# One small load moved to another queue, and the last projection partly issued earlier, in a decode-attention kernel limited by its loads

## The chip, the cores and the metric

The kernel runs on one core of a Trainium2 chip. The metric is device time of one execution in microseconds (us). A profiled execution also has a *span*, from the core's first to its last instruction; here the time is 1.8 to 1.9 us longer than the span throughout. In the record a run is *fast* or *slow*: slow when it is over 1.5% above the fastest of the same kernel. Engines: PE (TensorE), DVE (VectorE), ACT (ScalarE), POOL (GpSimd) and SP (SyncE, which here issues DMA transfers and computes nothing). PEld is PE's weight load, SPq and ACTq are the DMA issuing of SP and ACT.

## The reference

Eight tokens pass through two branches that a gate mixes. Branch A is attention with one query per token over the last 1,024 entries of a cache; branch B is a small MLP.

```python
q = (x @ wq) -> [8 tokens, 16 heads, 256]
k, v = last 1024 of the caches [8, 8 kv heads, 4096, 256], each for 2 query heads
o = softmax(q k^T / 16) v              # per token and head
a = o.reshape(8, 16 * 256) @ wo        # [4096, 448]
b = gelu(layernorm(x) @ w1 + b1) @ w2 + b2
g = sigmoid((x * gate_w).sum(-1))
out = g * a + (1 - g) * b              # [8, 448] bf16
```

All is bf16. Keys and values are 67 MB of the 77.7 MB that have to be read, so this is a kernel that reads memory.

## The kernel before

All large loads are issued by SyncE, in one order, into a ring of nine slots of 2 MB. `pump()` issues loads as long as slots are free; `done()` frees one. A unit `u` is four kv heads of one token; there are 16 units. For each, PE transposes the keys, computes scores, DVE and ACT do the softmax, PE multiplies by the values. At the start and the end the program says:

```python
x_sb = consts.tile([NB, D], BF16)
nc.sync.dma_start(x_sb[:], xf)         # 7 KB, first on SyncE
pump()                                 # nine slots; keys of unit 0 come first, in two halves
...
nc.scalar.dma_start(gw_b[:], ...)      # small constants on ScalarE
...
bring(u); values(u - 1)                # u = 15, the last unit
A_ps = ps_misc.tile([P, DQ], F32, ...); nc.vector.memset(A_ps[:], 0.0)
finish(u - 1)                          # head outputs 0-7 of token 7 complete
values(u); finish(u)                   # head outputs 8-15 of token 7
# "spread": 16 small matmuls bring all head outputs into the layout of wo's rows
for i in range(HPQ):
    for m in range(HPQ):
        nc.tensor.matmul(pp[32 * i : 32 * i + 32, m], lhsT=ident[:, m::HPQ], rhs=oTv[:, i], ...)
nc.vector.tensor_copy(oP[:], ...)
for q in range(NHQ):                   # projection with wo, 4 x 32 matmuls
    ...
nc.vector.scalar_tensor_tensor(res[:], in0=A_ps[:], ...)   # gate and mix
for i, (src, cols) in enumerate(quads(res)):               # four stores of 1.8 KB
    eng = nc.sync if i % 2 == 0 else nc.scalar
    eng.dma_start(out_f[:, cols], src)
```

wo's last quarter is loaded in three pieces, so that only the last 8 of 128 projection matmuls need the last bytes. The four stores alternate between SyncE and ScalarE, so SyncE's last two transfers are stores.

## Time and profile before

| | before |
|---|---|
| time, median of 3 (range) | 197.02 us (196.73 to 197.06) |
| span of the profiled run | 195.0 us |
| busy: PE, DVE, ACT | 76%, 58%, 43% |
| read by the large loads | 77.67 MB |
| share of DMA in the chain of waits | 96% |

From the page of the kernel before: granted PE clock (tenths), busy tenths of the 16 DMA engines, and what they moved, in 40 slices of 4.9 us.

```profile
...
PEclk9997566999999999999999999999999999999655
DMA  4999999999999999999999999999999999999940
GB/s 165 426 425 408 444 421 427 408 424 424 430 424 430 420 430 427 427 427 424 425 424 430 427 427 417 425 424 424 417 424 430 427 430 420 427 424 407 413 151 3
...
```

Read from left to right: after the first slice the DMA engines are full at about 425 GB/s up to the third last slice. In the second last the share drops to 4 tenths, and the last slice is empty. From the same page, the chain of work that ended last, by engine and by line:

```profile
...
DMA 96%; SPq 1%; issue 0%; PE 0%; DVE 0%
DMA slot<-in_A_k_cache_dram 58%; DMA slot<-in_A_v_cache_dram 20%; DMA slot<-in_A_wo_dram 10%; DMA slot<-in_A_wq_dram 7%; SPq L107 1%; SPq L123 1%; PE A_ps L562 0%; SPq L172 0%; DVE res L569 0%
...
```

From the last instruction backwards, each step is a landing of a large load that waited for the one before it. PE, DVE and ACT hardly occur in it.

The start in the timeline (start us, duration us, engine, line, operation, count):

```profile
...
0.73 0.58 ACTq L177 DMA_DIRECT2D gw_b<-in_gate_w_dram  x1
...
0.73 0.38 SPq L172 DMA_DIRECT2D x_sb<-in_A_x_dram  x1
...
1.17 1.27 SPq L107 DMA_DIRECT2D slot<-in_A_k_cache_dram  x2
...
```

x goes out first on SyncE, and the first key load 0.44 us later. The end in the timeline of the same run:

```profile
...
187.00 3.05 PE L562 MATMUL A_ps<-slot,oP 128*8 128x112 bf16 x120 [0.55 <-DVE oP L555]
190.27 0.36 PE L562 MATMUL A_ps<-slot,oP 128*8 128x112 bf16 x8 [0.22 <-DMA slot<-in_A_wo_dram]
...
190.68 0.33 DVE L569 SCALAR_TENSOR_TENSOR res<-A_ps,gg_s,mixb 128x112 bf16<-128x112 f32 x1 [3.73 <-PE A_ps L562]
191.04 1.05 SPq L579 DMA_DIRECT2D out_dram<-res  x2
191.04 0.67 ACTq L579 DMA_DIRECT2D out_dram<-res  x2
```

In the square brackets stands the idle time of the engine before the group, and what ended it. PE does 120 of the projection's matmuls, waits 0.22 us for the last bytes of wo, does the last 8; then DVE mixes, and SyncE and ScalarE store.

### The profile page before, as it was taken

The page shows a single profiled execution, that of the slowest core. Times are in us where ns is not written, and L with a number is a line of the kernel's source. Part 1 is how long each engine was busy: PE and PEld are TensorE (multiplying, and loading weights), DVE is VectorE, ACT ScalarE, POOL GpSimd, SP SyncE. Part 2 cuts the span into 40 slices and gives each one's busy share as a digit, 9 for nine tenths or more (in the row PEclk, how much of TensorE's full clock was granted, in tenths as well). Part 3 has the DMA queues.
Part 4 walks back from the last instruction along what each step waited for, and adds up shares of the span by engine and source line. Part 5 has one row for each costly group of instructions (what it writes and reads, how often), then busy time and mean ns, then how long its engine had stood idle before and what let it go on. Part 6 is the DMA issues. An engine that isn't in the chain of part 4 may idle for free.

```text
span 195.0 us, 5167 instructions
## 1 busy us (share of the span) xinstructions
PE 148.3 (76%) x2318; PEld 110.5 (57%) x2318; DVE 112.6 (58%) x258; ACT 82.9 (43%) x101; POOL 0.9 (0%) x7
## 2 busy tenths in 40 slices
PE   1399967887778787878767878778787878994780
PEld 0399927755565656564636464647373737553570
DVE  7531342867575757575738484847575757777210
ACT  2362003636373727272708181818282828562000
POOL 1000000000000000000000000000000000000000
PEclk9997566999999999999999999999999999999655
DMA  4999999999999999999999999999999999999940
GB/s 165 426 425 408 444 421 427 408 424 424 430 424 430 420 430 427 427 427 424 425 424 430 427 427 417 425 424 424 417 424 430 427 430 420 427 424 407 413 151 3
DMA packets 6744, 78.02 MB, mean 400 GB/s; under 512 B 945, under 2 KB 1346, under 8 KB 1986
## 3 DMA queue, kind: packets, MB, share of 16 engines
q1 hardware_dynamic: 6528, 77.67, 94.7%
q8 instruction: 18, 0.29, 0.6%
q10 hardware_dynamic: 194, 0.02, 0.1%
q14 instruction: 4, 0.03, 0.0%
HBM read 77.68 MB, written 0.01 MB: 398 GB/s over the span
## 4 chain that ended last, share of the span: by engine, by line
DMA 96%; SPq 1%; issue 0%; PE 0%; DVE 0%
DMA slot<-in_A_k_cache_dram 58%; DMA slot<-in_A_v_cache_dram 20%; DMA slot<-in_A_wo_dram 10%; DMA slot<-in_A_wq_dram 7%; SPq L107 1%; SPq L123 1%; PE A_ps L562 0%; SPq L172 0%; DVE res L569 0%
## 5 line engine op out<-in xcount | busy, mean ns | idle before, releaser
L325 ACT COPY kt<-ktp 128x1024 bf16<-128x1024 bf16 x64 | 63.2, 1017 | 82.1 <-PE ktp L322 82.1
L322 PE MATMUL ktp<-ident,slot 128*128 128x128 bf16 x1024 | 71.2, 226 | 21.6 <-ACT kt L325 10.9
L322 PEld LDWEIGHTS <-slot 128*128 128x128 bf16 x1024 | 64.8, 103 | 28.4 <-issue 15.6
L327 DVE COPY kt<-ktp 128x1024 bf16<-128x1024 bf16 x64 | 41.3, 685 | 16.0 <-PE ktp L322 16.0
L360 PE MATMUL S_ps<-kt,qw 128*8 128x512 bf16 x256 | 32.4, 627 | 0.3 <-DVE qw L351 0.3
L372 DVE TENSOR_REDUCE nmx<-S_ps 128x1 f32<-128x1024 f32 x16 | 19.6, 1225 | 22.4 <-PE S_ps L360 22.4
L388 DVE STREAM_TRANSPOSE EB<-E 128x1024 bf16<-128x1024 bf16 x16 | 19.9, 1245 | 6.3 <-ACT E L380 6.1
L420 PE MATMUL PO<-slot,ET 128*8 128x256 bf16 x512 | 17.6, 282 | 6.1 <-DVE ET L401 6.1
L380 ACT ACTIVATE E<-S_ps,nmx 128x1024 bf16<-128x1024 f32 x16 | 17.9, 1120 | 2.4 <-DVE nmx L373 2.4
L420 PEld LDWEIGHTS <-ET 128*8 128x8 bf16 x512 | 11.4, 88 | 10.3 <-DVE ET L401 8.4
L360 PEld LDWEIGHTS <-qw 128*8 128x8 bf16 x256 | 7.3, 95 | 12.0 <-issue 10.4
L401 DVE CAST ET<-sm 128x256 bf16<-128x256 f32 x16 | 6.7, 417 | 0.5 <-PE sm L399 0.5
L396 PE MATMUL sm<-EB,perm 128*128 128x256 bf16 x16 | 4.4, 273 | 1.6 <-DVE EB L388 1.6
L399 PE MATMUL sm<-selr,ones_f 128*128 128x8 f32 x32 | 5.3, 237 | 0.0
L440 DVE CAST oT<-sm 128x16 bf16<-128x16 f32 x16 | 3.5, 221 | 2.8 <-PE sm L437 2.8
L399 PEld LDWEIGHTS sm<-selr,ones_f 128*128 128x128 f32 x32 | 4.8, 188 | 0.1
L562 PE MATMUL A_ps<-slot,oP 128*8 128x112 bf16 x128 | 3.4, 295 | 0.8 <-DVE oP L555 0.5
L339 PE MATMUL qt<-xT,slot 128*128 128x8 bf16 x128 | 3.6, 168 | 0.4 <-DVE z L470 0.4
L339 PEld LDWEIGHTS <-slot 128*128 128x128 bf16 x128 | 3.6, 104 | 0.4 <-issue 0.3
L562 PEld LDWEIGHTS <-oP 128*8 128x8 bf16 x128 | 2.9, 121 | 1.2 <-DVE oP L555 0.7
L470 DVE TENSOR_TENSOR z<-hT,b_sb 128x112 f32<-128x112 f32 x1 | 0.3, 275 | 5.5 <-PE hT L460 5.5
L380 ACT ACTIVATION_READ_ACCUMULATOR E<-S_ps,nmx 128x1 f32 x16 | 3.2, 202 | 0.0
(122 smaller groups left out, 71.9 us busy)
## 6 DMA issues: line engine op xcount, KB each, us to landing
slot<-in_A_v_cache_dram SPq DMA_DIRECT2D x16, 2048.0 KB, 38.9
slot<-in_A_k_cache_dram SPq DMA_DIRECT2D x15, 2048.0 KB, 39.4
slot<-in_A_wo_dram SPq DMA_DIRECT2D x3, 896.0 KB, 32.0
slot<-in_A_k_cache_dram SPq DMA_DIRECT2D x2, 1024.0 KB, 7.1
slot<-in_A_wq_dram SPq DMA_DIRECT2D x1, 2048.0 KB
slot<-in_B_w_dram SPq DMA_DIRECT2D x1, 1568.0 KB
slot<-in_B_w_dram SPq DMA_DIRECT2D x1, 1344.0 KB, 9.8
slot<-in_A_wq_dram SPq DMA_DIRECT2D x1, 1024.0 KB
```

The costliest lines, as they stand in the source:

```text
L322: nc.tensor.transpose(ktp[:, c, :], kn[:, o : o + P], ident[:])
L325: nc.scalar.copy(dst, ktp[:])
L327: nc.vector.tensor_copy(dst, ktp[:])
L339: nc.tensor.matmul(qt[:, k, :], lhsT=w[:, o + c : o + c + P], rhs=xT[:, r + half, :], start=(r == 0 and k == 0), stop=(r == NR), skip_grou ...
L360: nc.tensor.matmul(S_ps[32 * a : 32 * a + RQ, hf * CH * SK : (hf + 1) * CH * SK], lhsT=qw[:, j, b, half, a, :], rhs=KT[hf][:, j, :, a::QUA ...
L372: nc.vector.reduce_max(nmx[:], S_ps[:], axis=AXIS.X, negate=True)
L380: nc.scalar.activation(E[:], S_ps[:], ACT.Exp, bias=nmx[:], scale=1.0, accum_out=rowsum[:])
L388: nc.vector.transpose(EB[:].rearrange("p c r -> p (c r)"), E[:])
L399: nc.tensor.matmul(sm[:, NCK, :], lhsT=ones_f[:], rhs=selr[:], start=True, stop=True)
L401: nc.vector.tensor_copy(ET[:], sm[:, 0:NCK, :])
L420: nc.tensor.matmul(PO[32 * t : 32 * t + RQ, :], lhsT=ET[:, c, 0:RQ], rhs=vn[:, c * Dh : (c + 1) * Dh], start=(c < QUAD), stop=(c >= NCK - ...
L562: nc.tensor.matmul(dst, lhsT=oP[:, j, q, :], rhs=w[:, o + cols.start : o + cols.stop], start=(q == 0 and j == 0), stop=(q == NHQ - 1 and j ...
```

## The change

Its intent: start the stream of loads earlier by taking x out of its queue, and take two waits of PE off the end by spreading and projecting the finished heads early.

```diff
     x_sb = consts.tile([NB, D], BF16)
-    nc.sync.dma_start(x_sb[:], xf)
     pump()
+    nc.scalar.dma_start(x_sb[:], xf)
...
     finish(u - 1)
-    values(u)
-    finish(u)
-    pp = ps_sm.tile(...)          # spread of all heads, one cast
...
+    def spread_rows(q0, q1): ...  # the same for a range of heads, pp from the ps_kt pool
+    def project(q): ...           # a quarter of the projection, as before
+
+    HALF = NHQ // 2
+    spread_rows(0, HALF)          # heads 0-7, complete by now
+    values(u)
+    finish(u)
+    project(0)
+    spread_rows(HALF, NHQ)
+    for q in range(1, NHQ):
+        project(q)
```

More of the change, by code (lines that the diff above doesn't have):

```diff
@@ L539, with spread_rows, project @@
     finish(u - 1)
-    values(u)
-    finish(u)
-    pp = ps_sm.tile([P, HPQ, NJ, NHQ, NB], F32, tag="sm", name="pp")
+    oP = consts.tile([P, NJ8, NHQ, NB], BF16)
     oTv = oT[:].rearrange("p (q i) j b -> p i j q b", i=HPQ)
-    for i in range(HPQ):
-        for m in range(HPQ):
-            nc.tensor.matmul(
-                pp[32 * i : 32 * i + 32, m],
-                lhsT=ident[:, m::HPQ],
-                rhs=oTv[:, i],
-                start=True,
-                stop=True,
-            )
-    oP = consts.tile([P, NJ8, NHQ, NB], BF16)
-    nc.vector.tensor_copy(oP[:], pp[:].rearrange("p m j q b -> p (m j) q b"))
-    for q in range(NHQ):
+    def spread_rows(q0, q1):
+        pp = ps_kt.tile([P, HPQ, NJ, q1 - q0, NB], F32, tag="ktp", name="pp")
+        for i in range(HPQ):
+            for m in range(HPQ):
+                nc.tensor.matmul(
+                    pp[32 * i : 32 * i + 32, m],
+                    lhsT=ident[:, m::HPQ],
+                    rhs=oTv[:, i, :, q0:q1, :],
+                    start=True,
+                    stop=True,
+                )
+        nc.vector.tensor_copy(
+            oP[:, :, q0:q1, :], pp[:].rearrange("p m j q b -> p (m j) q b")
+        )
+    def project(q):
         w = slot("wo", q - q % 2)
```

## The prediction

> **What bounds the kernel now.** The stream of big loads. The chain of waits is 96% DMA: keys 58%, values 20%, wo 10%, wq 7%. The queue table has 77.67 MB on the SyncE queue, 94.7% of sixteen engines' span; the page's slices show 9 tenths of DMA nearly throughout, near 425 GB/s[...]. PE is busy 76%, DVE 58%, ACT 43%; in the waits view PE waits 9.8 us for keys in 14 pieces, so it catches up with the loads again and again.
>
> So only three things can shorten the time: when the stream starts, how dense it is, and what follows its last byte.
>
> **Start.** In the timeline SyncE issues x at 0.73 us (0.38 us), and the first key half only at 1.17 us. The windows view shows no large traffic until 2.5 us. The change takes x out of this queue: the first key issue should move to 0.73 us, and the whole stream with it, by 0.44 us. x goes out at 0.73 us on ScalarE instead and should land at 2.0 to 2.8 us (PE first needs it at 2.38 us today). A few tenths of delay in the norm and the first transposes (9.0 us) are absorbed.
>
> **Tail.** Today the last wo bytes land at 190.23 us. PE ends the first 120 projection matmuls at 190.05 us, waits 0.22 us for DMA, then does the last 8 (0.36 us), then comes res (0.33 us), the output, and the end at 195.0. So PE has 0.2 us of slack: nearly critical, not quite. The change adds 16 small matmuls (16 took 0.45 us) and one cast (at most 0.42 us). It buys away two waits of PE after the last value product: 0.32 us for oT and 0.55 us for oP are covered by project(0) and project(1) (about 0.8 us each). Against that come a wait of some 0.3 us for oT ahead of the early spread, and its matmuls. Net I estimate PE 0.2 to 0.4 us earlier. The instruction order has only a quarter of the projection ahead of the second spread, after the last value product. PE's chain begins with the landing of the 15th key block (waited for at 160.78 us), so it moves with the stream. The end stays with DMA: the tail part is worth nothing, at most 0.1 us in runs in which PE happens to be last.
>
> **Sum.** 197.02 - 0.44 - (0 to 0.1) = 196.5 us, eight in ten between 196.1 and 196.95. Faster by over 2%: 0.01; within 2%: 0.98; slower: 0.01.
>
> **What would show it.** Right: first key issue near 0.73 us, big traffic from near 2.1 us; last wo landing near 189.8 us; PE's wait for wo before the last 8 matmuls above 0.3 us; landing to end unchanged (4.8 us). Wrong on the start: the stream begins earlier but the last landing does not. Wrong on the tail: PE has no wait for wo at the end.
>
> **What would make it wrong.** The granted clock falls to 0.5 at about 181 us; if it falls earlier, PE becomes last and eats the gain. The end is also uneven: the DMA share falls from 0.94 at 182 to 186 us to 0.12 at 189 to 190 us, so a few engines finish last, and anything that delays one of them by some tenths counts as much as the change. Runs of the same kernel differ by 0.3 us.

## The result, and the profile after

| | before | after |
|---|---|---|
| time, median of 6 (range) | 196.85 us (196.59 to 197.06) | 195.52 us (195.46 to 195.63) |
| span of the profiled run | 195.0 us | 193.7 us |

The ratio of the fast runs is 0.9933 (95% interval 0.992 to 0.9946). Here and below a ratio is the mean time of one kernel's fast runs over the mean of the other's in the same rounds, so it is not quite the ratio of the medians quoted. The gain is 1.33 us; I had predicted 0.44 to 0.54 us, and the time lies below my range. It is a small gain, but with six runs on either side and no overlap it is not noise.

From the page of the changed kernel, the clock and DMA lines and the chain that ended last:

```profile
...
PEclk9998559999999999999999999999999999999555
DMA  5999999999999999999999999999999999999950
...
DMA 82%; PE 9%; ACT 3%; DVE 2%; issue 1%; SPq 1%; ACTq 0%
...
```

DMA still fills the middle; in the third last slice the clock is 5 instead of 6 tenths. The chain is 82% DMA instead of 96%: from 160.7 us on, the landing of the 15th key block, it runs through PE, ACT and DVE, so in this run PE's work, not the last load, ended last, if only just: `res` starts 0.45 us after the last landing of wo, as before. That was one of the risks that I had named; the second trace below does not show it.

The start of the changed kernel in the timeline:

```profile
...
0.73 0.60 ACTq L173 DMA_DIRECT2D x_sb<-in_A_x_dram  x1
...
0.73 1.28 SPq L107 DMA_DIRECT2D slot<-in_A_k_cache_dram  x2
...
```

As predicted, the first key load is issued 0.44 us earlier. Two lines of the windows view show the traffic of it, first of the kernel before, then of the changed one (stretch and its length, busy time of PE, PEld, DVE, ACT and POOL with counts, clock, DMA share, GB/s):

```profile
...
2.00:3.00 1.00, 0.39 (x5) 0.31 (x5) 0.88 (x7) 0.98 (x1) 0.00 (x0) 1.00 0.63 132
3.00:6.00 3.00, 0.13 (x2) 0.04 (x1) 2.31 (x13) 0.67 (x3) 0.00 (x0) 1.00 0.95 373
...
```

```profile
...
2.00:3.00 1.00, 0.40 (x5) 0.32 (x5) 0.88 (x7) 0.60 (x1) 0.00 (x0) 1.00 0.92 229
3.00:6.00 3.00, 0.13 (x2) 0.04 (x1) 2.31 (x13) 1.05 (x3) 0.00 (x0) 1.00 0.98 402
...
```

Summed from the trace's packets, the changed kernel's loads are 0.19 MB ahead at 6 us, which at 425 GB/s is 0.45 us; from 9 us on and until 184 us the lead is 0.25 to 0.31 us (0.10 to 0.13 MB). The end of the changed kernel in the timeline:

```profile
...
187.97 2.46 PE L563 MATMUL A_ps<-slot,oP 128*8 128x112 bf16 x96
...
190.48 0.33 DVE L580 SCALAR_TENSOR_TENSOR res<-A_ps,gg_s,mixb 128x112 bf16<-128x112 f32 x1 [1.92 <-PE A_ps L563]
190.84 0.71 SPq L590 DMA_DIRECT2D out_dram<-res  x2
190.84 0.65 ACTq L590 DMA_DIRECT2D out_dram<-res  x2
```

DVE starts to mix at 190.48 instead of 190.68 us: 0.20 us of the 1.27 us by which the spans differ. The remaining 1.07 us come after it, in a part that the change does not touch. SyncE now issues its two stores in 0.71 us instead of 1.05 us. And they land sooner. In the waits view of SyncE, its wait for the stores at the program's end (us in total, times, longest), before and after:

```profile
...
SPq L605 <- DMA out_dram<-res: 1.8, 2, 1.2
...
```

```profile
...
SPq L616 <- DMA out_dram<-res: 1.1, 2, 0.9
...
```

Times of the two ends, from the trace's records (us from the span's start):

```
                                        before    after
last wo landing                         190.23   190.03
first SyncE store issued                191.04   190.84
idle between the two SyncE stores         0.43     0.04
second SyncE store issued               191.78   191.25
last packet of it, and last but one     193.06, 192.62    192.14, 192.11
8 KB instruction fetch (one packet)     192.76-193.07     192.61-193.12
last store landed                       193.92   192.64
end of the span                         194.95   193.68
```

So there are two new facts. In the kernel before, SyncE pauses 0.43 us between two stores, though `res`, from which it stores, was ready at 191.01 us and the first store had been issued from it at 191.04. And one of that store's eight data packets starts at 193.06 us, 0.44 us after the last of the seven others; a fetch of 8,192 bytes of instructions, on some DMA engine, ends at 193.07 us.

### The profile page after: what moved, and what is told of

It is laid out like the page before. It is cut to its first block, busy times and chain, and to the rows that moved or that the text cites. A ratio compares the mean times of both kernels' runs of the same rounds, so it can differ in the third digit from the quotient of the medians.

```text
span 193.7 us, 5200 instructions
## 1 busy us (share of the span) xinstructions
PE 148.1 (76%) x2334; PEld 110.3 (57%) x2334; DVE 112.9 (58%) x259; ACT 82.7 (43%) x101; POOL 0.8 (0%) x7
## 4 chain that ended last, share of the span: by engine, by line
DMA 82%; PE 9%; ACT 3%; DVE 2%; issue 1%; SPq 1%; ACTq 0%
DMA slot<-in_A_k_cache_dram 77%; DMA slot<-in_B_w_dram 5%; ACT kt L325 2%; PE S_ps L360 2%; PE ktp L322 2%; PE PO L420 2%; PE A_ps L563 2%; ACT E L380 1%; PE sm L437 1%; SPq L107 1%; DVE EB L388 1%; DVE nmx L372 1%; PE sm L399 0%; PE sm L396 0%; PE pp L547 0%
## 5 line engine op out<-in xcount | busy, mean ns | idle before, releaser
L322 PE MATMUL ktp<-ident,slot 128*128 128x128 bf16 x1024 | 70.2, 224 | 22.1 <-ACT kt L325 11.4
L322 PEld LDWEIGHTS <-slot 128*128 128x128 bf16 x1024 | 63.7, 102 | 29.0 <-issue 15.7
L420 PE MATMUL PO<-slot,ET 128*8 128x256 bf16 x512 | 18.5, 290 | 6.4 <-DVE ET L401 6.4
L420 PEld LDWEIGHTS <-ET 128*8 128x8 bf16 x512 | 12.2, 90 | 10.5 <-DVE ET L401 8.7
L339 PEld LDWEIGHTS <-slot 128*128 128x128 bf16 x128 | 3.6, 104 | 0.4 <-issue 0.3
L403 DVE RECIPROCAL rb<-sm 128x8 f32<-128x8 f32 x16 | 3.2, 199 | 0.0
```

The lines of the kernel that those rows point to most:

```text
L322: nc.tensor.transpose(ktp[:, c, :], kn[:, o : o + P], ident[:])
L339: nc.tensor.matmul(qt[:, k, :], lhsT=w[:, o + c : o + c + P], rhs=xT[:, r + half, :], start=(r == 0 and k == 0), stop=(r == NR), skip_grou ...
L420: nc.tensor.matmul(PO[32 * t : 32 * t + RQ, :], lhsT=ET[:, c, 0:RQ], rhs=vn[:, c * Dh : (c + 1) * Dh], start=(c < QUAD), stop=(c >= NCK - ...
```

## The experiments

The theories at the outset: **S**, the gain comes from x leaving the SyncE queue, by way of the stores at the end; **E**, it comes from the new order of the projection, which changes when the end falls. My prediction's own terms (0.44 us for the start, nothing for the projection) are tested by the same runs. All kernels gave correct results.

### 1 to 4: each part alone, and both kernels again

The head part alone (`e1_head_only`):

```diff
-    nc.sync.dma_start(x_sb[:], xf)
     pump()
+    nc.scalar.dma_start(x_sb[:], xf)
```

> Only the first part of the change: keys issued first, x on the ScalarE queue; the end of the kernel as before. Theory S (x leaving the SyncE queue frees the output stores at the end: in the profile before, the second SyncE store was issued 0.43 us after the first had finished issuing and its last packet landed at 193.92 us, 0.86 us after the others; in the profile after, neither happened): about 195.7 us, and a span of about 193.9. Theory E (the stores' delay comes from how the end of the kernel falls, so from the projection part): about 196.6 us, a fall of 0.3 us at most, the head start of the stream, with the late store still there.

The tail part alone (`e2_tail_only`) is the changed kernel with this undone.

> Only the second part: early spread and projection of the first quarter between the value product and the second spread; x on SyncE ahead of the keys as before. Theory S: about 196.7 us, the late second store still there. Theory E: about 195.7 us, no late store. My prediction had this part at 0 to 0.1 us.

Both kernels unchanged, for a second trace:

> The kernel before, unchanged, for a second trace. If the late second SyncE store (0.43 us gap between the two SyncE store issues, last packet 0.86 us after the others) belongs to the kernel and is not chance, it is here again and the span is about 195.0 us; if it is chance, the span may be 194.0.

> The changed kernel, unchanged, for a second trace. If the early end of the stores belongs to the kernel, the four stores are issued within 0.75 us and the end comes 2.9 us after the first is issued, again; span about 193.7 us. Open too: whether PE again has no wait for wo at the end (granted clock down to 0.5 from about 178 us).

| run | time, median (range) | ratio to before (95%) | gap between SyncE's stores | first store to last landing |
|---|---|---|---|---|
| head part alone | 195.50 (195.43 to 195.85) | 0.9935 (0.992 to 0.995) | 0.04 us | 1.81 us |
| tail part alone | 196.70 (196.61 to 196.87) | 0.9994 (0.9977 to 1.0011) | 0.46 us | 2.63 us |
| before, again | 197.07 (one run) | | 0.46 us | 2.72 us |
| after, again | 195.90 (one run) | | 0.04 us | 1.81 us |

(In the first profiled runs: before 0.43 and 2.88 us, after 0.04 and 1.81 us. The record calls the state of the two single runs unknown; their traces, not their times, are used below.) The stores in the timeline of the two halves, first the head part alone, then the tail part alone:

```profile
...
190.89 0.70 SPq L579 DMA_DIRECT2D out_dram<-res  x2
```

```profile
...
191.25 1.08 SPq L590 DMA_DIRECT2D out_dram<-res  x2
```

The gain is in the head part alone, as far as can be measured; none is measurable in the tail part. E has fallen. The slow end is not chance: of these six traces it is in all three with x on SyncE, and in none without.

### 5 to 7: is it the transfer of x, or the place of the store in SyncE's program?

Taking x off SyncE does two things: it removes a transfer from a queue, and it makes SyncE's instruction stream shorter by one (89 records of SyncE in the trace after, 90 before). Counted from 0 in the built program, SyncE's second store is number 80 in the kernel before, and number 79 with x on ScalarE. Theory **P**: the number counts, because something at a fixed place in SyncE's instruction stream, between 79 and 80, holds it up (this place is called the boundary below). Theory **Q**: the transfer counts. A drain on SyncE (an instruction with no DMA, placed after the first nine slots of loads) separates the two.

```diff
     nc.scalar.dma_start(x_sb[:], xf)
+    nc.sync.drain(fusable=False)       # e5_head_drain1: one; e6_head_drain2: two
```

> The head part alone (195.5 us) plus one drain on SyncE after its first nine slots of loads: one instruction more in SyncE's program, no DMA[...]. SyncE's second store is then again its instruction number 80, as in the kernel before (79 with the head part alone). Theory P (what counts is the place of the last store in SyncE's instruction stream): the gap of 0.4 us between the two SyncE stores is back, and a late last packet, about 196.5 us. Theory Q (what counts is the x transfer itself on the SyncE queue[...]): no gap, 195.5 us.

> The same with two drains. Theory P in the form of a boundary in the instruction stream just ahead of number 80: the boundary now falls ahead of the first store, where SyncE waits over 10 us for the result anyway, so the gap is hidden and the time is back at about 195.5 us. If instead every further instruction costs, about 196.5 us or more. Theory Q: 195.5 us.

```diff
     nc.sync.dma_start(x_sb[:], xf)     # the kernel before
     pump()
+    nc.sync.drain(fusable=False)       # e7_before_drain1
```

> The kernel before, x on SyncE first, plus one drain on SyncE: nothing but one instruction added. Theory P with the boundary: the stores come without the gap and the kernel is faster by about 1 us, 195.8 us; what is left against the head part alone (195.5 us) is the worth of the earlier start of the stream, 0.25 to 0.44 us. Theory Q: no change, 196.8 us, or slower.

| run | number of 2nd store | time, median (range) | ratio to before (95%) | gap | 8 KB fetch | first store to last landing |
|---|---|---|---|---|---|---|
| head, one drain | 80 | 196.78 (196.48 to 196.88) | 1.0003 (0.9986 to 1.002) | 0.44 | 192.43-192.76 | 2.59 us |
| head, two drains | 81 | 196.00 (195.66 to 196.13) | 0.9959 (0.9944 to 0.9974) | 0.06 | 183.93-184.26 | 1.81 us |
| before, one drain | 81 | 195.91 (195.87 to 196.04) | 0.9958 (0.9943 to 0.9973) | 0.06 | 184.30-184.63 | 1.81 us |

The stores in the timeline of the three runs, in this order:

```profile
...
190.99 1.12 SPq L580 DMA_DIRECT2D out_dram<-res  x2
```

```profile
...
191.53 0.71 SPq L581 DMA_DIRECT2D out_dram<-res  x2
```

```profile
...
191.30 0.67 SPq L580 DMA_DIRECT2D out_dram<-res  x2
```

P holds and Q has fallen. One idle instruction more undoes the gain; two bring most of it back; and the kernel before becomes 0.9 us faster by an instruction that does nothing. The fetch marks the same place. Counted in each trace's own records of SyncE (which leave out branches), it begins 1.06 to 1.41 us after the end of the 79th record (the first store in the kernel before), whatever that record is, and 3.6 to 3.8 us after it in the two runs with number 81, in which the stream of loads is still running. With the second store at 79 the boundary comes after the stores, where SyncE waits for their landing anyway (in the changed kernel the fetch begins at 192.61 us, the last store lands at 192.64). At 80 it comes between the two stores: there SyncE pauses (0.43 us in the kernel before), and the fetch itself, from 192.76 to 193.07 us there, falls among the packets of the second store, from 192.56 to 193.08. At 81 the boundary lies ahead of the first store, where SyncE has to wait for the result anyway (11.2 and 10.7 us in its waits view); the fetch is then seen at about 184 us.

In all four traces with number 80 (before twice, tail alone, head with one drain) the last packet of the second store starts when the fetch ends, to 0.01 us: 193.06 and 193.07, 193.42 and 193.42, 193.15 and 193.16, 192.76 and 192.76. In the others the store's packets have gone before the fetch begins, or (number 81) the fetch ended some 8 us ahead of them. So the cost has at least two parts: SyncE's pause of 0.43 to 0.46 us, and the meeting with the fetch that comes with the pause (the last packet starts 0.12 to 0.44 us after the last of the others, at most 0.03 us without it). A third part has no explanation here: the landing is seen 0.69 to 0.83 us after the end of the last packet, against 0.48 to 0.56 us in the other traces. Together, from first store to last landing, 2.59 to 2.88 us against 1.79 to 1.83 us in the nine other traces of normal speed, 0.9 us in the mean.

I had expected 195.5 us for two drains, and got 196.0. In both runs with number 81 the fetch now lies inside the stream of loads, and wo landed late, at 190.71 and 190.57 us. That the fetch delayed the stream is a possible reason; no run tests it.

### 8, 9, 11, 12: what is the earlier start worth by itself?

A partner with the late start but the good end: x first on SyncE, and the first keys as one load, so that the second store is number 79 (`e8_x_first_k0_one`).

```diff
-    add_kv("k", A_k_cache, 0, parts=2)
+    add_kv("k", A_k_cache, 0)
```

> x first on SyncE as in the kernel before, so the stream starts as late as there (large traffic from 2.5 us), but the first key block is one load of 2 MB instead of two of 1 MB, so SyncE's second store is its instruction number 79. It has the late start and should have the undisturbed end. Theory P: no gap between the stores, the 8 KB instruction fetch of some 0.3 us after them, time 195.5 to 195.95 us. The distance to the head part alone, run beside it, is what the earlier start is worth by itself: 0.4 us if the lead of 0.3 to 0.45 us in bytes reaches the end, about 0 if it is lost in the last microseconds. Theory Q (x on the SyncE queue is what disturbs the end): 196.8 us.

> The head part alone again, in five rounds, as the partner of the run with x first and one key load: 195.5 us.

A second partner, with SyncE's program as in the head part alone (`e11_head_held`): GpSimd writes zeros into a corner of the first slot, and the first key load waits for it.

```diff
         def load(t):
+            if parts > 1:
+                nc.gpsimd.memset(t[:, 0:256], 0.0)
             n = NCK * Dh // parts
```

> The head part alone, with the first key load held back by about 0.3 to 0.5 us: GpSimd first writes zeros to a corner of the slot, and SyncE's first load has to wait for it. Same instructions on SyncE, same order, x on ScalarE, undisturbed end expected (stores without gap). Only the start of the stream differs from the head part alone, run beside it. If the earlier start is worth what its lead in bytes says, this is slower by 0.3 to 0.45 us; if the lead is lost at the end, the two are equal within 0.1 us. Profiled landings so far put it at 0.25 us.

> The head part alone once more, as the partner of the held one in the same rounds: 195.5 to 195.8 us.

| pair in the same rounds | late start | early start | difference by ratios |
|---|---|---|---|
| second store number 79, keys as one load | 196.31 us, 0.9971 | 195.81 us, 0.9955 | 0.3 us |
| number 79, first load held | 196.18 us, 0.9963 | 195.51 us, 0.9930 | 0.65 us |
| number 80 (before; head with one drain) | 196.76 us | 196.78 us, 1.0003 | 0.0 us |
| number 81 (before with one drain; head with two) | 195.91 us, 0.9958 | 196.00 us, 0.9959 | 0.0 us |

(The difference is that of the two ratios to the kernel before, times 196.8 us. By the spread of the executions each has a standard error of 0.09 to 0.16 us.) So the first pair is barely told from zero; the second is, but at 0.65 us it is more than the 0.34 us by which the load was held, so not all of it can be the start. Both late partners missed what I had expected of them: 195.5 to 195.95 us for the first, 0.3 to 0.45 us slower for the second. The held load was issued at 1.07 instead of 0.73 us. One of its five executions, the profiled one, took 620 us, with key transposes of 699 ns in the mean where they otherwise take 226 ns; it counts as slow and is left out, and why it happened is not known. For the issue time alone I use its trace. The run with one key load was not clean: in its trace PE ran last, with no wait for wo (`res` starts 0.55 us after the last landing of wo instead of 0.45), so some 0.1 us of its 0.3 us may be PE's.

So the earlier start is worth something between nothing and 0.65 us, depending on the rest. The traces give a more even picture. In six traces with the early start and no fetch inside the stream the last wo bytes land at 190.03 to 190.37 us, in the mean at 190.21; in three with the late start (before twice, tail alone) at 190.23 to 190.63, in the mean at 190.43. That is 0.22 us, but the two ranges overlap, and with so few traces it is an indication and no more (the run with one key load, late too, landed at 190.55). Of the lead that the stream keeps until 184 us (0.29 to 0.42 us in these six traces), some six tenths arrive by these means. Why the timed pairs with number 80 and 81 show nothing of it stays open; with the errors above, noise may be enough.

### 10: a still earlier start

If the start counts, ScalarE may issue the second half of the first keys at once (`e10_two_queues`):

```diff
             for i in range(parts):
-                nc.sync.dma_start(
+                eng = nc.sync if i == 0 else nc.scalar
+                eng.dma_start(
```

> The head part, with the second half of the first key block issued by ScalarE at 0.73 us, ahead of x, while SyncE issues the first half: the ramp at the start should be shorter (the page's bytes by 4 us were 0.54 MB with the head part alone; up to 0.2 MB more), worth up to 0.4 us if a lead reaches the end, nothing if it does not. SyncE's last store is its number 78: if the boundary lies ahead of number 80, the end stays undisturbed. So 195.1 to 195.5 us; above 196.3 us would speak against theory P.

It took 197.07 us (ratio 1.0013, 1.0 to 1.0025), 1.3 us more than the head part alone in the same rounds (195.81 us). By my own words a time above 196.3 us would speak against P, so the trace has to say where the time went. The stores were undisturbed, as P says (gap 0.04 us, fetch after the stores, first store to last landing 1.83 us). But the boundary had only moved: after the 79th record, here the first of SyncE's two waits for the stores at the program's end (number 80 by the built program, as a branch has number 79), SyncE pauses 0.45 us again, 0.28 us of it after the landing that the next wait needs (193.49 us). The span ends 1.33 us after the last landing, 1.02 to 1.11 us in the other twelve traces of normal speed. That is another sign for P, and some 0.3 us of the loss. SyncE's first issues in its timeline show where the rest began:

```profile
...
0.73 0.65 SPq L108 DMA_DIRECT2D slot<-in_A_k_cache_dram  x1
1.44 1.04 SPq L124 DMA_DIRECT2D slot<-in_B_w_dram  x2
10.81 1.28 SPq L124 DMA_DIRECT2D slot<-in_A_wq_dram  x3
...
```

After three transfers SyncE waits until 10.81 us (3.26 us with the head part alone). SyncE's waits view of this run puts the wait down to a landing of keys, with 8.3 us as the longest of the four on its line:

```profile
...
SPq L124 <- DMA slot<-in_A_k_cache_dram: 21.5, 4, 8.3
...
```

The second half of the first keys, on ScalarE's queue, landed at 10.80 us, 0.01 us before SyncE went on. So by the trace a load of wq on one queue waited for a landing on the other; by what means was not shown.

With little queued, less was moved. The windows view of that stretch, first the head part alone, then this run:

```profile
...
6.00:14.00 8.00, 5.77 (x63) 5.51 (x64) 3.92 (x14) 3.92 (x5) 0.00 (x0) 1.00 1.05 441
...
```

```profile
...
6.00:14.00 8.00, 0.52 (x5) 0.35 (x5) 2.16 (x12) 0.00 (x0) 0.00 (x0) 1.00 0.96 356
...
```

441 against 356 GB/s for 8 us is 0.68 MB, or 1.6 us of the stream at 425 GB/s; some 0.5 us of it were won in the stretches before and after. (x, queued behind the second half of the keys on ScalarE, came late too: PE first used it at 11.37 instead of 2.39 us.) At the last landing of wo 0.5 us of the delay are left (190.85 us, 190.37 us in the partner's trace). So no experiment beat the changed kernel. The head part alone equals it (195.50 to 195.81 us in three sets of rounds).

## Why the prediction was wrong

- *Bound by the stream of loads*: right. The chain of the kernel before is 96% DMA, and no reordering on PE moved the time (tail part alone: 0.9994).
- *Start: the first key issue moves by 0.44 us, and the stream with it*: right for the issue (1.17 to 0.73 us) and for the lead at 6 us (0.45 us). *The last landing should move by as much*: too much; 0.20 us in the first pair of traces, 0.22 us in the mean, with overlapping ranges. I had named the uneven end as a risk: the DMA share fell from 0.94 to 0.12 over the last 8 us, so a few engines end last.
- *Tail: worth nothing, at most 0.1 us*: right, 0.12 us by medians, not told from zero. *PE's wait for wo grows to over 0.3 us*: wrong in the first trace, in which PE had no wait at all: the clock fell to half at 178.8 instead of 181.3 us, and the next-to-last value product took 1.88 instead of 1.05 us. In the second trace it fell at 180.4 us and PE did wait (0.61, 0.23 and 0.22 us), though before the last 8 matmuls no longer than in the kernel before (0.22 us). What sets the time of that fall was not shown: the clock records have only full and half clock (1.00 and 0.50), and the fall near the end came between 177.7 and 181.9 us in the thirteen traces of normal speed.
- *Landing to end unchanged (4.8 us)*: **this is the step that failed.** It was 4.72 us before (190.23 to 194.95) and 3.65 us after (190.03 to 193.68). I took the end as a fixed cost because the change does not touch it. But the change made SyncE's instruction stream one shorter, and so moved its last store to the near side of the boundary between 79 and 80. By the traces this is worth 0.9 us in the mean and 1.07 us in the first pair; with the 0.20 us by which the result was ready earlier it makes up the 1.27 us between the spans.

The sign was in the profile that I had: 1.05 us for SyncE's two stores beside 0.67 us for ScalarE's. An issue that takes longer on one queue than on its twin asks for an explanation.

What is shown and what is argued: that the place in SyncE's instruction stream decides, that the gap and the late packet come and go with it, and that the late packet starts as the fetch ends, is shown. That in the pause of 0.43 to 0.46 us SyncE waits for its next instructions is inference from these and from the pause that moved to another place in run 10, and not shown: the trace has no record for the pause, and none of the engine for which the 8,192 bytes were fetched.

## What to carry to other kernels

When a kernel's end is a chain of small stores, look at each queue's issue times there: here a pause of 0.43 to 0.46 us at a fixed place in SyncE's instruction stream fell between its last two stores, and with it the stores took 0.9 us longer to land; adding or removing a single instruction earlier on that queue moved the place. So do not credit an unrelated edit with such a gain before a run with a neutral instruction in its place has told the two apart. And look at what a bulk transfer on a second queue does to the first queue's loads: in the failed attempt above SyncE issued its first load of wq at 10.81 instead of 3.26 us.
